# The last quad of w_out's sums on VectorE and its stores on ScalarE; the first weight split behind the third pair's even terms

## The chip, the cores and the metric

One core of a Trainium2 chip runs the whole kernel. The metric is the time of one execution on the device in microseconds. TensorE (PE) multiplies matrices; VectorE (DVE), ScalarE (ACT) and GpSimd (POOL) work on elements; SyncE (SP) and ScalarE issue most of the DMAs. Each engine takes its instructions in the order in which they were written; between engines there are semaphores.

## The reference

```python
B, H, S, D = 8, 8, 576, 64
scores = q @ k.T / sqrt(D)                 # per batch and head
ret = scores * Dmat[h]                     # Dmat = gamma[h] ** (i - j) for i >= j, else 0
x = (ret @ v).transpose(0, 2, 1, 3).reshape(4608, 512)
g, val = x @ w_gate, x @ w_val             # 512 -> 1536
out = (silu(g) * val) @ w_out              # 1536 -> 512, all float32
```

## The kernel before, in words

**Attention.** The 64 heads of all batches are worked in 32 pairs, each in chunks of 64 positions with a carried state. A `tick(t)` has TensorE's instructions for three pairs at once: `own_values(t-2)` (L481) needs the masked scores `ret` of pair t-2, `new_states(t-1)` is L490, `earlier_values(t-2)` (L500, L504) needs the carried states, and `scores(t-1)` (L511, L517) needs the transposed queries and keys, qT and kT. VectorE and ScalarE then do the element work of the tick, in this order: `even` (a copy, L528) and the scaling of keys (L459), the outputs of pair t-2 into x (`to_x`, L554 and L568), `ret` (L524), the last row of it (L532), the states (L534 to L539), qT and kT of pair t (L454). For the first four pairs (`hi == HP` in `tick`) the order is a little different: in a tick come scores and new states of pair t-1, then `masked(t-1)` with `even`, `ret` and states, then the values and outputs of pair t-2, then the transposes of pair t by TensorE (L440).

**Feed-forward network.** Tokens come in a first tile of 512 (`up0`, L650, and `down0`, L662) and four tiles of 1024. The tiles of 1024 use a fast scheme for products of 4 x 4 blocks with 26 multiplications and prepared sums: `up_step` (L870) runs 26 steps for each of three quads of the hidden dimension, `down_step` (L909) 26 steps. The sums of blocks of x are made by VectorE (`x_sums`), those of the up weights by GpSimd in the second tile (`w_sums` and `first_sums`), and each of these is then stored to DRAM from ScalarE's queue (L873), so that later tiles read it back. The operands of `down_step` are sums of blocks of w_out: `out_sums(qd)` makes them for quad `qd`, 24 sums of 128x256 by the table `OUT_SUMS`, and stores 26 blocks to the DRAM tensors `dn0` to `dn25` (L728). A sum is written to one of `sum_places` and its place comes free when its last use, often the store, is over. The places of quad 2 of w_out and some of `sum_places` are later used for the sums of x.

**Weights.** Weights are loaded as they are, 64-bit float numbers, into three raw buffers; `split` (ScalarE, L378 and L379) and `rounding` (VectorE, L391 and L392) turn a half of each into float32. `rounding(j)` calls `split(j + 1)`, and `split` issues the load of a further weight.

**Order around the change.** First come ticks 0 to 5 with the first `split` and `rounding`. Then a list `plan` merges `up0`, ticks 4 to 9, weight loads and the first groups of `out_sums` (a group is the sums for three stores). Then twelve `down0`, with tick 10 after the second, 11 after the fourth, 12 after the seventh and 13 after the ninth, and the remaining groups of `out_sums`: one after each of the first three `down0`, two after each later one. After the ninth, `first_sums(0, 0, 4)` makes the first sums of the up weights. Then `out0` copies the first tile's output and stores it from ScalarE's queue (L670), and the `up_step`s of the second tile begin. Before the change all sums of w_out are GpSimd's and all their stores are SyncE's.

A DMA increments one of eight completion semaphores. They are taken in turn by the DMAs of both queues, and a DMA is issued only when the one before it on its semaphore has landed.

Of the kernel before, what the change touches and what calls it, by code (L numbers as in the profile page):

```python
# [154 lines left out]
def kernel(  # L155
# [32 lines left out]
    nc = tc.nc  # L188
# [13 lines left out]
    TB = TW // 4  # L202
    NF = DF // P
    NQ = NF // 4
# [37 lines left out]
    rest = const.tile([P, 17920], F32, name="rest")  # L242
    raw_at, part_at, x0_at, dn_at, sum_at = 0, 6144, 8192, 10240, 16384
# [125 lines left out]
    def split(j):  # L369

        i, f = halves[j]
        bits = bits_of(i, f)
        top, ulp = [rest[:, part_at + 512 * (2 * n + j % 2) : part_at + 512 * (2 * n + j % 2 + 1)] for n in range(2)]
        blocks = lambda a: a.rearrange("p (c m) -> p c m", m=P)
        nc.scalar.activation(out=blocks(top), in_=bits[:, :, :, 1].bitcast(F32), func=AF.Prelu, scale=2.0 ** -112, alpha=2.0 ** 32)  # L378
        nc.scalar.activation(out=blocks(ulp.bitcast(I32)), in_=bits[:, :, :, 0].bitcast(U32), func=AF.Copy, scale=2.0 ** -29)  # L379
        parts[j] = top.bitcast(I32), ulp.bitcast(I32)  # L380
        if f and j // 2 + RAWS < len(order):
            load_w(j // 2 + RAWS)

    def rounding(j):

        i, f = halves[j]
        dst = weights[i][1][f].bitcast(I32)
        top, ulp = parts.pop(j)  # L390
        nc.vector.tensor_scalar(out=dst, in0=top, scalar1=3, scalar2=None, op0=ALU.logical_shift_left)  # L391
        nc.vector.tensor_tensor(out=dst, in0=dst, in1=ulp, op=ALU.add)  # L392
        if j + 1 < len(halves):
            split(j + 1)
# [200 lines left out]
    def tick(t, lo=HP, hi=NP, spread=False, then=None):  # L595
        go_on(len(pieces))
        if hi == HP:

            if lo <= t - 1 < hi:
                scores(t - 1, True)  # L600
                new_states(t - 1)
                for f in masked(t - 1):
                    f()
            if lo <= t - 2 < hi:
                own_values(t - 2)
                earlier_values(t - 2)
                to_x(t - 2)[0]()
            for f in transposes(t) if lo <= t < hi else ():
                f()
            return  # L610
        if lo <= t - 2 < hi:
            own_values(t - 2)
        if lo <= t - 1 < hi:
            new_states(t - 1)
        if lo <= t - 2 < hi:
            earlier_values(t - 2)
        if lo <= t - 1 < hi:
            scores(t - 1, t - 2 < lo)
        copies, *masks = masked(t - 1) if lo <= t - 1 < hi else (lambda: None,)
        keys, *new = transposes(t) if lo <= t < hi else (lambda: None,)  # L620
        outputs = to_x(t - 2)[0] if lo <= t - 2 < hi else lambda: None
        if t - 2 >= 0 and light(t - 2):
            pieces.append(lambda: (copies(), keys(), outputs()))
        else:
            pieces.extend([lambda: (copies(), keys()), outputs])
        pieces.extend(masks)
        pieces.extend(new)
        if then:
            pieces.append(then)
        if not spread:  # L630
            go_on(len(pieces))
# [33 lines left out]
    def out0():  # L665
        for i, bank in enumerate(banks):
            o = rest[:, part_at + 512 * i : part_at + 512 * (i + 1)]
            (nc.vector.tensor_copy if i > 1 else nc.scalar.copy)(out=o, in_=bank)
        for i in range(4):
            nc.scalar.dma_start(out=out[i * P : (i + 1) * P, :], in_=rest[:, part_at + 512 * i : part_at + 512 * (i + 1)])  # L670
# [5 lines left out]
    def add(eng, op, view, to=None):  # L676
        dst, srcs = view(int(op[1])) if to is None else to, [view(int(a)) for a in op[2:]]
        if op[0] == "neg":
            eng.tensor_scalar(out=dst, in0=srcs[0], scalar1=-1.0, scalar2=None, op0=ALU.mult)
        elif op[0] == "nad" and eng is nc.vector:  # L680
            eng.scalar_tensor_tensor(out=dst, in0=srcs[0], scalar=-1.0, in1=srcs[1], op0=ALU.mult, op1=ALU.subtract)
        elif op[0] == "nad":
            eng.tensor_tensor(out=dst, in0=srcs[0], in1=srcs[1], op=ALU.add)
            eng.tensor_scalar(out=dst, in0=dst, scalar1=-1.0, scalar2=None, op0=ALU.mult)
        else:
            eng.tensor_tensor(out=dst, in0=srcs[0], in1=srcs[1], op=ALU.add if op[0] == "add" else ALU.subtract)  # L686

    up_ops = [[dr.tile([P, 512], F32, name=f"up{qd}_{i}") for i in range(N)] for qd in range(NQ)]
    dn_ops = [dr.tile([P, 768], F32, name=f"dn{i}") for i in range(N)]

    sum_places = [rest[:, sum_at + TB * i : sum_at + TB * (i + 1)] for i in range(6)]
    more_places = [rest[:, raw_at + TB * i : raw_at + TB * (i + 1)] for i in range(16) if i % 4]

    events = []
    for line in OUT_SUMS:
        i, s = line.split("|")
# [2 lines left out]

    def out_sums(qd):

        place = {}

        def view(s):
            return w_dn[:, qd, s // 2, s % 2] if s < 8 else place[s]

        def used(e):
            return [e[1]] if e[0] is None else [int(a) for a in e[1][2:]]  # L710

        def release(k):

            for s in list(place):
                for e in events[k + 1 :]:
                    if s in used(e):
                        break
                    if s == e[0]:
                        sum_places.append(place.pop(s))
                        break  # L720
                else:
                    sum_places.append(place.pop(s))

        def do(k):
            e = events[k]
            if e[0] is None:
                _, slot, i = e
                nc.sync.dma_start(out=dn_ops[i][:, qd * TB : (qd + 1) * TB], in_=view(slot))  # L728
            else:
                new = sum_places.pop(0)  # L730
                add(nc.gpsimd, e[1], view, new)
                if e[0] in place:
                    sum_places.append(place[e[0]])
                place[e[0]] = new
            release(k)

        r, ends = [], [k for k, e in enumerate(events) if e[0] is None]
        for g in range(0, N, 3):
            lo, hi = ends[g - 1] + 1 if g else 0, ends[min(g + 2, N - 1)] + 1

            def group(lo=lo, hi=hi):
                for k in range(lo, hi):
                    do(k)

            r.append(group)
        return r
# [188 lines left out]

    for t in range(HP + 2):
        tick(t, 0, HP)
        if t == 2:
            split(0)

        for j in {2: (0,), 3: (1, 2), 4: (3, 4, 5)}.get(t, ()):
            rounding(j)
        if t == 3:
            load(HP)
        if t > 3:
            for f in range(2):
                up0(f, range(2) if t == 4 else range(2, HP))
# [6 lines left out]
        if t + AHEAD < NP:  # L954
            load(t + AHEAD)

    groups = [(qd, group) for qd in range(NQ) for group in out_sums(qd)]
    todo = [m for m in range(3, len(order))]
    plan = []

# [7 lines left out]
    for f in range(2, NF):  # L968
        round_until({4: 12, 6: 13, 8: 14, 9: 15, 10: 16, 11: 17}.get(f, f + 2))
        plan.append(lambda f=f: up0(f, range(HP)))  # L970
        if f - 1 in tick_at and f < NF - 1:
            plan.append(lambda t=tick_at[f - 1]: next_load(t))
        if f in tick_at:
            plan.append(lambda t=tick_at[f]: tick(t, HP, FIRST))
        if f >= NF - 2:

            plan.append(lambda t=tick_at[f]: next_load(t))
        for _ in range(0 if f == 9 else 3):
            if f >= (7, 10, NF)[groups[0][0]]:
                if f + 1 == NF and more_places:  # L980
                    plan.append(lambda places=more_places[:]: sum_places.extend(places))
                    more_places.clear()
                plan.append(lambda group=groups.pop(0)[1]: group())
    assert not todo
# [3 lines left out]
    for m, f in enumerate(down_order):  # L988
        down0(f)
        go_on(4)  # L990
        if m in tick_at:
            tick(tick_at[m], HP, FIRST, tick_at[m] + 1 < needed(1))
            go_on(1)
        if m == 8:
            first_sums(0, 0, 4)
        if m > 8:
            x_sums(1, 3 * (m - 9), min(3 * (m - 8), X_FIRST), True)
        for _ in range(min(1 if m < 3 else 2, len(groups))):
            groups.pop(0)[1]()
    out0()  # L1000
    x_sums(1, X_FIRST, X_FIRST_OF_ALL, True)
    done = FIRST
# [55 lines left out]
```

## Time and profile before

| | |
|---|---|
| median of 8 runs | 1079.23 us (1076.23 to 1083.83) |
| the profiled execution | 1083.83 us, of which the profile spans 1082.1 |
| TensorE busy | 1043.3 us (96%) |
| VectorE, ScalarE, GpSimd busy | 652.6, 271.5, 415.3 us |
| granted TensorE clock | 0.99 in the mean |
| DMA | 198.58 MB, 184 GB/s in the mean |

A row of the profile names the line, the engine, the operation, what is written and read, the number of instructions, then times. "SPq" and "ACTq" are DMA issues of SyncE and ScalarE. In a timeline the two numbers at the start are the start and the duration in microseconds from the start of the span, and the bracket at the end is the idle time before and what ended it. A row of several instructions has the start of the first.

### The profile page before, as it was taken

Reading aid. Unit: us, or ns where it says so; the run is one execution under the profiler, and the core shown is the slowest. Engines: PE = TensorE matmul, PEld = TensorE weight load, DVE = VectorE, ACT = ScalarE, POOL = GpSimd, SP = SyncE. Lnnn points to the kernel's source line nnn. Section 1 sums busy time; section 2 is a strip of 40 time slices with the busy share of each in tenths; the row PEclk is TensorE's granted clock in tenths of the full one; section 3 lists DMA queues with packets and bytes.
Section 4 is the critical chain, followed back from the end, with each engine's and each line's share of the span. In section 5 each row is a group of like instructions: output and inputs, shape, how many; then the busy total and the mean of one; then the engine's idle time right before and its main releaser. Section 6 shows DMA issues by size and latency. Waiting matters only on the chain.

```text
span 1082.1 us, 21481 instructions
## 1 busy us (share of the span) xinstructions
PE 1043.3 (96%) x8420; PEld 854.5 (79%) x8420; DVE 652.6 (60%) x1069; ACT 271.5 (25%) x578; POOL 415.3 (38%) x372
## 2 busy tenths in 40 slices
PE   6899999699999999999999999999999999999998
PEld 5445555488788788888888888888888888888887
DVE  4468755567879766754646869535267465244644
ACT  3355400124333211223232111122221012231110
POOL 5002359676464402741315025622151375122505
PEclk9999999799999999999999999999999999999999
DMA  9699774766576868767657778554564555555653
GB/s 260 179 279 240 211 189 143 216 190 187 158 209 184 251 143 247 213 180 196 154 165 214 180 204 231 155 152 135 153 177 150 161 177 154 154 149 159 184 162 98
DMA packets 300700, 198.58 MB, mean 184 GB/s; under 512 B 215352, under 2 KB 244056, under 8 KB 300600
## 3 DMA queue, kind: packets, MB, share of 16 engines
q1 hardware_dynamic: 268230, 159.16, 54.2%
q10 hardware_dynamic: 31954, 37.17, 10.4%
q8 instruction: 67, 1.10, 0.4%
q0 software_dynamic: 416, 0.89, 0.3%
q14 instruction: 33, 0.27, 0.1%
HBM read 157.04 MB, written 40.11 MB: 182 GB/s over the span
## 4 chain that ended last, share of the span: by engine, by line
PE 79%; POOL 6%; DMA 5%; DVE 5%; issue 2%; SPq 2%; ACT 1%; ACTq 0%; DVEq 0%; POOLq 0%
PE bankC L870 11%; PE bankB L870 11%; PE bankE L870 10%; PE bankA L870 10%; PE bankA L909 6%; PE bankE L909 6%; PE bankB L909 6%; PE bankC L909 6%; POOL rest L686 3%; DVE rest L810 2%; PE bankA L650 2%; PE bankC L650 2%; PE bankE L650 2%; PE bankB L650 2%; PE outer L504 1%
## 5 line engine op out<-in xcount | busy, mean ns | idle before, releaser
L810 POOL TENSOR_TENSOR rest<-rest 128x512 f32<-128x512 f32 x56 | 79.2, 1420 | 300.9 <-DVE rest L810 282.8
L885 ACT ACTIVATE io<-rest 128x256 f32<-128x256 f32 x180 | 75.0, 416 | 341.1 <-DVE rest L810 291.6
L870 PE MATMUL bankA<-rest,arena 128*128 128x256 f32 x544 | 130.6, 383 | 4.4 <-ACT rest L807 3.3
L870 PE MATMUL bankC<-rest,arena 128*128 128x256 f32 x544 | 129.2, 380 | 1.1 <-POOL arena L839 0.6
L686 POOL TENSOR_TENSOR arena<-arena 128x512 f32<-128x512 f32 (+1 forms) x72 | 115.2, 1612 | 28.2 <-DMA up<-arena 20.4
L870 PE MATMUL bankE<-rest,arena 128*128 128x256 f32 x512 | 122.6, 383 | 0.8 <-DVE rest L810 0.8
L686 POOL TENSOR_TENSOR rest<-rest 128x256 f32<-128x256 f32 (+1 forms) x86 | 81.4, 969 | 105.9 <-issue 64.8
L870 PE MATMUL bankB<-rest,arena 128*128 128x256 f32 x512 | 121.4, 380 | 0.4 <-DVE rest L810 0.4
L870 PEld LDWEIGHTS bankA<-rest,arena 128*128 128x128 f32 x544 | 103.8, 192 | 20.9 <-issue 5.5
L892 POOL TENSOR_TENSOR arena<-rest,io 128x256 f32<-128x256 f32 x72 | 52.0, 729 | 166.9 <-ACT io L885 166.9
L870 PEld LDWEIGHTS bankC<-rest,arena 128*128 128x128 f32 x544 | 102.8, 190 | 16.2 <-issue 1.2
L870 PEld LDWEIGHTS bankE<-rest,arena 128*128 128x128 f32 x512 | 98.0, 192 | 14.9 <-issue 1.1
L870 PEld LDWEIGHTS bankB<-rest,arena 128*128 128x128 f32 x512 | 96.9, 190 | 14.3 <-DVE rest L810 0.8
L810 DVE TENSOR_TENSOR rest<-bankB,rest 128x512 f32<-128x512 f32 x72 | 48.9, 687 | 66.2 <-PE bankB L870 48.2
L810 DVE TENSOR_TENSOR rest<-bankE,rest 128x512 f32<-128x512 f32 x72 | 48.8, 686 | 64.7 <-PE bankE L870 46.1
L810 DVE TENSOR_TENSOR rest<-bankC,rest 128x512 f32<-128x512 f32 x72 | 48.9, 687 | 63.4 <-PE bankC L870 43.5
L810 DVE TENSOR_TENSOR rest<-bankA,rest 128x512 f32<-128x512 f32 x72 | 48.8, 686 | 61.1 <-PE bankA L870 43.8
L888 DVE SCALAR_TENSOR_TENSOR arena<-rest,io 128x256 f32<-128x256 f32 x84 | 58.6, 702 | 11.7 <-ACT io L885 11.7
L909 PE MATMUL bankA<-arena 128*128 128x256 f32 x252 | 58.0, 380 | 1.3 <-DVE arena L686 1.3
L909 PE MATMUL bankB<-arena 128*128 128x256 f32 x252 | 58.3, 381 | 0.0
L909 PE MATMUL bankC<-arena 128*128 128x256 f32 x252 | 58.1, 380 | 0.0
L909 PE MATMUL bankE<-arena 128*128 128x256 f32 x252 | 57.9, 379 | 0.0
(179 smaller groups left out, 1630.1 us busy)
## 6 DMA issues: line engine op xcount, KB each, us to landing
arena<-up SPq DMA_DIRECT2D x234, 256.0 KB
arena<-dn SPq DMA_DIRECT2D x104, 384.0 KB
up<-arena ACTq DMA_DIRECT2D x78, 256.0 KB
dn<-rest SPq DMA_DIRECT2D x78, 128.0 KB
out_dram<-rest SPq DMA_DIRECT2D x32, 256.0 KB
qk<-in_q_dram SPq DMA_DIRECT2D x108, 72.0 KB
qk<-in_k_dram SPq DMA_DIRECT2D x108, 72.0 KB
v<-in_v_dram SPq DMA_DIRECT2D x58, 128.0 KB
```

The costliest lines, as they stand in the source:

```text
L504: nc.tensor.matmul(xr[half[hl]] if c + 1 == NC else xo[half[hl ^ c % 2 * exchange(i)], c // 2, c % 2], state[half[hl], c, :], s["qT"][half ...
L650: nc.tensor.matmul(bank, w_up[:, f // 4, gv, f % 4, c // 2, (c % 2) * P : (c % 2 + 1) * P], xs[0][:, c, :], start=(c == 0), stop=(c == HP ...
L686: eng.tensor_tensor(out=dst, in0=srcs[0], in1=srcs[1], op=ALU.add if op[0] == "add" else ALU.subtract)
L810: eng.tensor_tensor(out=at(op[1]), in0=at(op[2]), in1=at(op[3]), op=ALU.add if op[0] == "add" else ALU.subtract)
L870: nc.tensor.matmul(b[:, gv * TB : (gv + 1) * TB], w[:, gv, ts(c, P)], rhs[:, c, :], start=(opens and gv == 0 and c == 0), stop=(c == 1), s ...
L885: nc.scalar.activation(out=s, in_=src[:, 0:TB], func=AF.Silu, scale=-1.0 if negative else 1.0)
L888: return lambda: nc.vector.scalar_tensor_tensor(out=dst, in0=src[:, TB : 2 * TB], scalar=-1.0, in1=s, op0=ALU.mult, op1=ALU.mult)
L892: nc.gpsimd.tensor_tensor(out=dst, in0=src[:, TB : 2 * TB], in1=s, op=ALU.mult)
L909: nc.tensor.matmul(b[:, m * TB : (m + 1) * TB], lhs[:, qd, ts(m, P)], w[:, qd], start=(opens and qd == 0 and m == 0), stop=(qd == NQ - 1), ...
```

## The change

Two things are changed. First, `out_sums` of the last quad (`NQ - 1`) makes its sums on VectorE, into six places of its own, and stores them from ScalarE's queue; a group of it is placed after each of the first nine `down0`, and one group of the other quads after each `down0` while there are any. GpSimd gets six further places at the end of the plan, where it got twelve. Second, `split(0)` and `rounding(0)` stand in tick 3, behind `masked(2)`, and no longer at the end of tick 2. VectorE has three instructions fewer for a quad than GpSimd: a negated sum is one instruction there and two on GpSimd. The numbers of lines behind L603 grow by 3 to 7.

```diff
@@ tick, first four pairs
                 new_states(t - 1)
                 for f in masked(t - 1):
                     f()
+            if t == 3:
+                split(0)
+                rounding(0)
             if lo <= t - 2 < hi:
                 own_values(t - 2)
@@
-    sum_places = [rest[:, sum_at + TB * i : sum_at + TB * (i + 1)] for i in range(6)]
+    pool_places = [rest[:, sum_at + TB * i : sum_at + TB * (i + 1)] for i in range(6)]
     more_places = [rest[:, raw_at + TB * i : raw_at + TB * (i + 1)] for i in range(16) if i % 4]
+    vector_places = more_places[6:]
@@ out_sums
         place = {}
+        eng, queue, sum_places = ((nc.vector, nc.scalar, vector_places) if qd + 1 == NQ else (nc.gpsimd, nc.sync, pool_places))
@@ do
-                nc.sync.dma_start(out=dn_ops[i][:, qd * TB : (qd + 1) * TB], in_=view(slot))
+                queue.dma_start(out=dn_ops[i][:, qd * TB : (qd + 1) * TB], in_=view(slot))
             else:
                 new = sum_places.pop(0)
-                add(nc.gpsimd, e[1], view, new)
+                add(eng, e[1], view, new)
@@ first ticks
         tick(t, 0, HP)
-        if t == 2:
-            split(0)
-
-        for j in {2: (0,), 3: (1, 2), 4: (3, 4, 5)}.get(t, ()):
+
+        for j in {3: (1, 2), 4: (3, 4, 5)}.get(t, ()):
             rounding(j)
@@ plan
-    groups = [(qd, group) for qd in range(NQ) for group in out_sums(qd)]
+    groups = [(qd, group) for qd in range(NQ - 1) for group in out_sums(qd)]
+    last_groups = out_sums(NQ - 1)
@@
-                    plan.append(lambda places=more_places[:]: sum_places.extend(places))
+                    plan.append(lambda places=more_places[:6]: pool_places.extend(places))
@@ after each down0
-        for _ in range(min(1 if m < 3 else 2, len(groups))):
+        if groups:
             groups.pop(0)[1]()
+        if last_groups:
+            last_groups.pop(0)()
```

## The prediction

> **What bounds the kernel now.** I read the busy rows first (TensorE 96% of the span), then TensorE's own waits, since only its idle time can be won, then the stages, then each engine's timeline around the widest gap. TensorE's waits from 140 to 230 us:
>
> ```profile
> PE bankC L870 <- POOL arena L686: 7.0, 1, 7.0
> PE bankA L870 <- ACT rest L807: 3.3, 1, 3.3
> PE bankC L870 <- POOL arena L839: 0.6, 1, 0.6
> PE outer L511 <- DVE kT L454: 0.2, 1, 0.2
> ```
>
> Three gaps, 10.9 us, all at L870: the first ten steps of `up_step` for the second x tile. The table of stages shows what they cost (busy us and count of PE, PEld, DVE, ACT, POOL, then the granted clock, DMA share and GB/s):
>
> ```profile
> 138.00:150.00 12.00, 12.00 (x162) 6.35 (x160) 3.25 (x12) 1.15 (x2) 2.75 (x4) 1.00 1.15 227
> 150.00:176.00 26.00, 25.57 (x382) 14.86 (x382) 14.52 (x38) 0.00 (x0) 23.17 (x32) 1.00 0.50 164
> 176.00:187.00 11.00, 11.00 (x29) 5.16 (x28) 10.86 (x15) 1.17 (x2) 10.92 (x11) 1.00 0.37 124
> 187.00:220.00 33.00, 22.09 (x78) 17.50 (x77) 18.43 (x25) 6.01 (x13) 22.08 (x23) 0.79 0.72 211
> ```
>
> TensorE idles 10.91 us from 187 to 220 at a clock of 0.79, while from 150 to 176 it is full, GpSimd too (23.17 of 26), VectorE half empty and ScalarE empty. TensorE's timeline gives the loss:
>
> ```profile
> 187.86 1.89 PE L870 MATMUL bankB<-rest,arena 128*128 128x256 f32 x8
> 196.76 3.78 PE L870 MATMUL bankC<-x_odd,arena 128*128 128x256 f32 x8 [7.01 <-POOL arena L686]
> 206.86 3.41 PE L870 MATMUL bankA<-rest,arena 128*128 128x256 f32 x8 [3.33 <-ACT rest L807]
> 219.72 1.99 PE L870 MATMUL bankC<-rest,arena 128*128 128x256 f32 x8 [0.57 <-POOL arena L839]
> ```
>
> Step 0 starts at 186.14 and step 10 at 219.72: 33.6 us for ten steps, which follow each other every 1.73 us where nothing waits (17.3). So **16.3 us** are lost, 10.9 of waits and the rest in groups of eight that take 3.4 to 3.8 us after them. Why GpSimd is late:
>
> ```profile
> 177.12 8.85 POOL L686 TENSOR_TENSOR rest<-rest 128x256 f32<-128x256 f32 x8
> 195.45 2.93 POOL L686 TENSOR_TENSOR arena<-arena 128x512 f32<-128x512 f32 x2
> ```
>
> It is at the w_out sums until 195.45, and only then makes the weight sum that step 2 needs. The sums of quad 2 begin after quad 1's last, at about 172.4. The 3.3 us gap is ScalarE: its stores of the first output wait until 197.29 for a completion semaphore that SyncE's queue of w_out stores holds (data ready at 184.4), and step 0's bank is copied behind them.
>
> [...] eight GpSimd sums take 5.83 us at 156.6 and 8.85 at 177.1, where VectorE adds in SBUF without pause, and VectorE's 128x512 adds then take 1.2 us against 0.68 alone.[...] Here a w_out store lands in 1.9 us (issued 201.16, releases VectorE at 203.08) to 3.6 us (issued 148.33, releases GpSimd at 152.01, where the DMA share is over 1).[...]
>
> **The change by parts.** (1) Off GpSimd: quad 2's 24 sums, 27 instructions there, 172.4 to 196, 23.8 us. Off SyncE: 26 of the 60 stores that fill its queue from 147.53 to 202.58, so its next loads (202.68) start some 20 us earlier, beside TensorE's full stage and not in the up-steps. The weight sum of step 2 then follows quad 1 (about 173 to 178), long before 190; the stores of the first output no longer wait. What is late next is the chain store of step 0's weight, its landing, then six GpSimd sums to step 10. That store can be issued some 2.1 us after step 0 starts; the 3.1 us landing of 205.22, 5.5 of 206.57 and sums of 1.45 put step 10 at 17.5 us after step 0 against 17.3. **Gain 16.1 us.**
>
> (2) On VectorE: 24 instructions. An add of 128x256 there takes 0.41 us (L891), 0.9 where GpSimd competes; I take 0.77, half of a GpSimd sum of 0.72 longer. In sum 10 to 18 us, against VectorE's waits between 137.9 and 176 of 5.1, 3.1, 0.6, 0.9, 5.7 and 4.6 us (20.0). As work alone it fits. But VectorE runs in order, and the change puts *waits* ahead of pair work. Six places serve 24 sums, so the seventh waits for the first store to land, and it stands before `to_x(8)`, `ret` and states of pair 9, kT of pair 10:
>
> ```profile
> 147.10 1.12 ACTq L301 DMA_DIRECT2D vl<-in_v_dram  x1
> 149.28 0.22 DVE L532 TENSOR_TENSOR ret_last<-outer,last_near 128x64 f32<-128x64 f32 x1
> 151.86 0.73 DVE L454 STREAM_TRANSPOSE kT<-qk 128x576 f32<-128x576 f32 x1
> 152.65 0.27 PE L511 MATMUL outer<-qT,kT 64*64 64x64 f32 x2 [0.20 <-DVE kT L454]
> ```
>
> TensorE waits for kT already here, by 0.2 us: no slack. ScalarE is at pair loads until 148.22, so the first store lands at 148.3 + 3.6 = 151.9. Then: sum 0.4, outputs 0.9, `ret` and its last row 0.75 (153.95, against 149.4), states 2.8 (between 1.9 with GpSimd idle and 3.1 beside it), qT 0.7, four more sums that stand between qT and kT 3.1, kT 0.7: 161.2. TensorE starts the scores at 161.2 and not 152.65: **loss 8.5 us**. Ends: landing 1.9 and sums of 0.41 give 157.1, loss 4.5; landing 4.6 (seven stores in flight together) and sums of 0.9 give 10.5.
>
> Tick 12 is covered: TensorE reaches it at 163.87 + 8.5 = 172.4, and its pair work, five sums later, is done by about 172. Tick 13 is not. Before its `ret(11)` stand four sums; one waits for a ScalarE store whose completion semaphore was last used by one of SyncE's stores at the end of quad 1. Quad 1 ends at 172.4 now; 13 VectorE sums meet it, at (8.85 - 5.83)/8 = 0.38 each, so 177; SyncE's store 1.9 and ScalarE's 0.45 + 1.9 give 181.3, the sum 0.4, outputs and `ret` 1.7: 183.4. TensorE arrives at 173.66 + 8.5 = 182.2: 1.2 us, and 1.3 more for the states. **Loss 2.5 us**, ends 0 and 6. The clock:[...] I take nothing; upper end 3.4.
>
> (3) ScalarE's 26 stores at 0.45 us are 12 us in a queue that has no work from 149.4 to 183.76; behind them are a weight negation and the copies of the first output, needed at 194 then. Nothing, unless the last stores slip beyond 194; the end would be 3 us. GpSimd keeps 12 of its 18 places for two thirds of its sums, which costs nothing as long as the 1.9 us landings hold.
>
> (4) `split(0)` and `rounding(0)` move from tick 2 to tick 3 behind `masked(2)`. ScalarE copies `even` at 21 and not 24.63, since no weight is awaited before it; VectorE's pair terms come some 3 us earlier, its first rounding some 3 us later (21.3 to 24), the next two about 2 earlier, still before L650 needs them at 34.65. SyncE's weight load (30.23) and pair loads behind it go out up to 1.7 us earlier. TensorE:
>
> ```profile
> 28.43 0.57 PE L481 MATMUL outer<-ret,v 64*64 64x64 f32 x23 [0.95 <-DVE rest L568]
> 32.01 0.35 PE L481 MATMUL outer<-ret,v 64*64 64x64 f32 x9 [3.01 <-issue]
> ```
>
> The 0.95 us goes, but the next gap stands within 32 equal matmuls and waits for no data: "issue". I hold that it ends at the same time, so 0; ends 1.5 gained if it moves along, 1 lost if the earlier loads delay it.
>
> **Sum:** -16.1 + 8.5 + 2.5 + 0 = -5.1 us. The profiled execution took 1083.83 (span 1082.1, 1.7 around it), so 1078.7; it was the slowest of eight, and the median 1079.23 becomes **1074.1**.
>
> **Rivals.** *A, full cover:* the stores land fast, VectorE's gaps take all: 1079.2 - 15.7 = 1063.5. For it, 20 us of gaps; against it, the order: the waits stand ahead of kT. *B, slower:* VectorE held by stores. With 3.6 us for every landing the second stall is about 7 us, the first 9.5, and two half-clock windows bring 3.4: 19.9 against 16.1, 1083.0. It decides from the point where stalls in ticks 11 to 13 exceed 16.1 us. Against it, the 1.9 us landings once the loads are over. *C, equal:* stalls of 13 to 19 us return what is won, 1079.
>
> **Numbers.** A measurement of this kernel can tell about 0.3% (3.2 us) from no change. Forecast 0.56 (1070 to 1078, a sixth of it within 0.3%), A 0.16, B 0.14, C 0.14. Faster 0.47 + 0.16 = 0.63, same 0.09 + 0.14 = 0.23, slower 0.14. The range leaves out the best half of A and the worst of B: 1065 to 1082.
>
> **What would show it.** Right: TensorE has no gap at the first L870 groups, all at 1.9 us; a gap of 4.5 to 10.5 us at L481, L504 and L511 near 150 to 161, released by VectorE, a smaller one near 182; VectorE waits for DMA stores; step 0 at about 197. Wrong: no gap near 150 (A), one over 6 us near 182 or a clock under 1 from 150 to 185 (B), a new wait for GpSimd or ScalarE after step 0, or a start that moves TensorE's first L650 from 34.65 by over 1 us.

## The result, and the profile after

The changed kernel takes **1073.49 us** in the median of 21 runs (1070.52 to 1078.34), the kernel before beside it 1079.41 in 58: ratio **0.9947, interval 0.9935 to 0.9958**, 5.7 us less (7.0 to 4.5). The forecast was 1074.1. The profiled execution took 1070.52 us, its span is 1068.8. It is the fastest of its runs as the profile of before is one of the slowest, so the two spans differ by 13.3 us where the medians differ by 5.9: of the two traces only stretches are compared below, not spans.

TensorE's waits from 140 to 230 us in the profile after (total, times, longest):

```profile
PE outer L481 <- DVE ret_last L532: 5.0, 1, 5.0
PE outer L511 <- DVE kT L454: 2.3, 1, 2.3
PE outer L500 <- PE outer L481: 0.2, 1, 0.2
```

The three gaps at the up-steps (L870, now L876) are gone, and two others have come, both in tick 11 and both ended by VectorE. The stages, in the same columns as those of before:

```profile
138.00:150.00 12.00, 6.98 (x24) 2.87 (x26) 4.15 (x14) 0.00 (x0) 2.76 (x4) 0.91 1.01 264
150.00:176.00 26.00, 23.69 (x304) 14.25 (x301) 21.07 (x43) 0.00 (x0) 19.88 (x25) 0.78 0.64 203
176.00:187.00 11.00, 10.82 (x90) 5.47 (x89) 8.36 (x21) 1.15 (x2) 3.26 (x2) 1.00 0.96 217
187.00:220.00 33.00, 33.00 (x140) 26.23 (x139) 26.41 (x36) 9.93 (x20) 16.64 (x12) 1.00 0.53 174
```

The idle time and the low clock have moved from the last row (before: 22.09 busy, clock 0.79) to the first two. The up-steps are full at clock 1.00. TensorE's timeline, with steps 0, 2 and 10:

```profile
192.27 1.89 PE L876 MATMUL bankA<-rest,arena 128*128 128x256 f32 x8
...
195.73 1.89 PE L876 MATMUL bankC<-x_odd,arena 128*128 128x256 f32 x8
...
209.79 1.99 PE L876 MATMUL bankC<-rest,arena 128*128 128x256 f32 x8
```

Ten steps take 209.79 - 192.27 = 17.5 us. GpSimd's timeline shows why:

```profile
168.93 1.45 POOL L689 TENSOR_TENSOR arena<-arena 128x512 f32<-128x512 f32 x1
183.74 1.58 POOL L689 TENSOR_TENSOR arena<-arena 128x512 f32<-128x512 f32 x1 [13.37 <-DVE arena L689]
```

It is through with quad 1 at 168.93 and makes a weight sum then (before: 195.45, step 2 waiting for it), and the gap behind it is a wait for VectorE. What VectorE does with the work, in its timeline:

```profile
147.29 0.79 DVE L689 TENSOR_TENSOR rest<-rest 128x256 f32<-128x256 f32 x1 [3.71 <-DMA dn<-rest]
...
148.93 0.68 DVE L524 TENSOR_TENSOR ret<-inner,near 128x512 f32<-128x512 f32 x1
...
152.55 2.97 DVE L689 TENSOR_TENSOR rest<-rest 128x256 f32<-128x256 f32 x4
155.45 0.77 DVE L454 STREAM_TRANSPOSE kT<-qk 128x576 f32<-128x576 f32 x1
```

A sum waits 3.71 us for a store to land and holds `ret` behind it, and four sums of 0.74 us stand between qT and kT. And TensorE's timeline where it waits, with the first groups behind it:

```profile
149.79 1.14 PE L481 MATMUL outer<-ret,v 64*64 64x64 f32 x32 [5.02 <-DVE ret_last L532]
...
156.26 0.37 PE L511 MATMUL outer<-qT,kT 64*64 64x64 f32 x2 [2.31 <-DVE kT L454]
...
157.53 2.07 PE L665 MATMUL bankA<-rest,arena 128*128 128x512 f32 x2
...
162.19 1.02 PE L665 MATMUL bankE<-rest,arena 128*128 128x512 f32 x2
```

The group of L665 at 157.53 takes 2.07 us where the one at 162.19 takes 1.02: the two waits are paid a second time in half-clocked work. The granted clock is 0.50 from 147.91 to 161.56, for 13.65 us. In quarters of that length, with one ahead and one behind and the columns of the stages:

```profile
144.50:147.91 3.41, 0.27 (x1) 0.00 (x0) 0.62 (x1) 0.00 (x0) 0.83 (x2) 1.00 0.97 324
147.91:151.33 3.42, 1.54 (x56) 1.54 (x60) 3.31 (x12) 0.00 (x0) 3.25 (x5) 0.50 0.61 203
151.33:154.74 3.41, 2.63 (x56) 2.26 (x48) 3.38 (x7) 0.00 (x0) 3.41 (x5) 0.50 0.68 225
154.74:158.15 3.41, 1.89 (x37) 1.64 (x38) 1.94 (x4) 0.00 (x0) 3.33 (x5) 0.50 0.71 235
158.15:161.56 3.41, 3.41 (x5) 1.35 (x4) 3.41 (x11) 0.00 (x0) 3.32 (x5) 0.50 0.47 158
161.56:164.98 3.42, 3.42 (x9) 1.52 (x8) 3.31 (x8) 0.00 (x0) 3.25 (x6) 1.00 0.71 234
```

It falls after a stretch in which TensorE is busy for 0.27 us, within the first wait, and comes back after one in which it is busy for all 3.41 us.

### The profile page after: what moved, and what is told of

It reads as the page before. It is cut to its first block, busy times and chain, and to the rows that moved or that the text cites. A ratio compares the mean times of both kernels' runs of the same rounds, so it can differ in the third digit from the quotient of the medians.

```text
span 1068.8 us, 21457 instructions
## 1 busy us (share of the span) xinstructions
PE 1038.6 (97%) x8420; PEld 851.2 (80%) x8420; DVE 663.5 (62%) x1093; ACT 272.0 (25%) x578; POOL 395.7 (37%) x345
## 3 DMA queue, kind: packets, MB, share of 16 engines
q10 hardware_dynamic: 35698, 40.58, 11.4%
## 4 chain that ended last, share of the span: by engine, by line
PE 87%; DVE 5%; DMA 4%; issue 1%; POOL 1%; ACT 1%; SPq 0%; ACTq 0%; DVEq 0%; POOLq 0%
PE bankC L876 11%; PE bankE L876 11%; PE bankB L876 11%; PE bankA L876 11%; PE bankA L915 6%; PE bankB L915 6%; PE bankC L915 6%; PE bankE L915 6%; DVE rest L816 2%; PE bankA L653 2%; PE bankC L653 2%; PE bankE L653 2%; PE bankB L653 2%; PE outer L504 2%; PE outer L481 2%
## 5 line engine op out<-in xcount | busy, mean ns | idle before, releaser
L876 PE MATMUL bankC<-rest,arena 128*128 128x256 f32 x544 | 129.2, 380 | 0.5 <-DVE rest L816 0.5
L876 PE MATMUL bankA<-rest,arena 128*128 128x256 f32 x544 | 129.0, 380 | 0.5 <-DVE rest L816 0.4
L876 PE MATMUL bankE<-rest,arena 128*128 128x256 f32 x512 | 121.5, 380 | 0.8 <-DVE rest L816 0.8
L876 PE MATMUL bankB<-rest,arena 128*128 128x256 f32 x512 | 121.4, 380 | 0.4 <-DVE rest L816 0.4
L876 PEld LDWEIGHTS bankA<-rest,arena 128*128 128x128 f32 x544 | 102.9, 190 | 16.0 <-issue 1.3
L876 PEld LDWEIGHTS bankC<-rest,arena 128*128 128x128 f32 x544 | 102.8, 190 | 15.6 <-issue 1.2
L876 PEld LDWEIGHTS bankE<-rest,arena 128*128 128x128 f32 x512 | 96.8, 190 | 14.7 <-issue 1.2
L876 PEld LDWEIGHTS bankB<-rest,arena 128*128 128x128 f32 x512 | 97.0, 190 | 14.3 <-DVE rest L816 0.8
L689 POOL TENSOR_TENSOR rest<-rest 128x256 f32<-128x256 f32 (+1 forms) x66 | 65.8, 1018 | 100.7 <-issue 60.1
L894 DVE SCALAR_TENSOR_TENSOR arena<-rest,io 128x256 f32<-128x256 f32 x84 | 58.2, 698 | 11.7 <-ACT io L891 11.7
```

Of the source, the lines that this page charges most:

```text
L876: nc.tensor.matmul(b[:, gv * TB : (gv + 1) * TB], w[:, gv, ts(c, P)], rhs[:, c, :], start=(opens and gv == 0 and c == 0), stop=(c == 1), s ...
L894: return lambda: nc.vector.scalar_tensor_tensor(out=dst, in0=src[:, TB : 2 * TB], scalar=-1.0, in1=s, op0=ALU.mult, op1=ALU.mult)
```

## The experiments

The theory: the up-steps win 16 us because GpSimd is free, and tick 11 loses 11 of it because VectorE's sums, waiting for a place and standing ahead of kT, come before TensorE's operands. The first rival: most of the 5.7 us is the other edit, the later split. To compare runs I take two stretches from TensorE's timeline, which begin over 100 us behind the start: **A** from the start of the last `down0` group (bankE) ahead of tick 11 to the start of up-step 0, and **B** from step 0 to step 10.

| kernel | A, us | B, us | A + B less before's | measured by ratio, us |
|---|---|---|---|---|
| before (mean of 4 traces) | 37.1 | 33.5 | 0 | 0 |
| the change | 48.5 | 17.5 | -4.6 | -5.7 (-7.0 to -4.5) |
| e1 sums and stores only | 49.2 | 17.5 | -3.9 | -2.8 (-4.6 to -1.0) |
| e2 split only | 36.5 | 34.6 | +0.5 | -0.9 (-2.8 to +1.1) |
| e3 twelve places | 43.0 | 18.0 | -9.6 | -11.2 (-14.0 to -8.3) |
| e4 no stores | 45.0 | 17.5 | -8.1 | -12.4 (-15.3 to -9.6) |
| e5 twelve places, kT first | 40.5 | 18.2 | -11.9 | -13.9 (-16.4 to -11.4) |
| e6 six places, kT first | 49.7 | 18.2 | -2.7 | -5.0 (-6.4 to -3.7) |
| e7 stores on SyncE | 63.4 | 17.5 | +10.3 | +7.8 (+5.5 to +9.9) |
| e9 as e5, sums two groups later | 41.2 | 17.7 | -11.7 | -13.2 (-16.6 to -9.7) |

The last column is the ratio less one, times 1079.5 us; the other columns come from one trace each. The traces of before have 37.1 and 33.6, 36.4 and 34.1, 37.6 and 33.0, 37.2 and 33.5.

**e1, one half of the change.** All of the sums, places and stores; the split stays in tick 2.

```diff
-            if t == 3:
-                split(0)
-                rounding(0)
...
+        if t == 2:
+            split(0)
-        for j in {3: (1, 2), 4: (3, 4, 5)}.get(t, ()):
+        for j in {2: (0,), 3: (1, 2), 4: (3, 4, 5)}.get(t, ()):
```

(against the changed kernel)

> Only the sums and stores of the last quad are moved; the first split stays in tick 2. Theory of the prediction (all of the change's effect lies between tick 11 and up-step 10, the start is worth nothing): ratio to before 0.995, as for the whole change; first L650 group at 34.6 us as before, gap of some 5 us at L481 after tick 10 and 2 us at L511, no gap at the first up-steps. Rival (the 4.8 us by which the changed kernel's profile is ahead at its first L653 come from the split's place): this part alone gives what is left, 0.998 to 1.000.

Measured: 1077.3 us, ratio 0.9974 (0.9957 to 0.9991). B is 17.5 us as with the whole change, and tick 11 has gaps of the same kind (4.9, 0.7 and 2.9 us). So the gain at the up-steps and the loss at tick 11 belong to this half. The ratio lies nearer the rival's 0.998 than the theory's 0.995, which its interval leaves out: the whole change gains 2.9 us more than this half, though the intervals reach 1.8 and 1.2 us to either side.

**e2, the other half**, against the kernel before.

```diff
+            if t == 3:
+                split(0)
+                rounding(0)
...
-        if t == 2:
-            split(0)
-        for j in {2: (0,), 3: (1, 2), 4: (3, 4, 5)}.get(t, ()):
+        for j in {3: (1, 2), 4: (3, 4, 5)}.get(t, ()):
```

> Only the first split and rounding are moved to tick 3; the sums are all GpSimd's as before. Theory of the prediction: 1.000, within 1.5 us, the gap of 3 us that is put down to issue within L481 still there near 32 us. Rival (the split's place gives the 4.8 us at the start): 0.995 to 0.997, first L650 group near 30 us and no gap within L481.

Measured: 1077.99 us, ratio 0.9992 (0.9974 to 1.0010): alone it can't be told from nothing. The up-steps keep their gaps (8.1 and 5.0 us). e1 and e2 together say only that the later split is worth between 0 and about 3 us; e8, e10 and e11 go on with that.

**e3, twelve places for VectorE**, none of them handed to GpSimd. No store has to land before the thirteenth sum.

```diff
-    vector_places = more_places[6:]
+    vector_places = more_places[:]
...
-                if f + 1 == NF and more_places:
-                    plan.append(lambda places=more_places[:6]: pool_places.extend(places))
-                    more_places.clear()
```

> The changed kernel, but VectorE's sums have twelve places and GpSimd keeps its first six (they took six and twelve), so VectorE's first twelve sums wait for no store. Theory (the loss at tick 11 is the wait for the first store, with what is queued behind it): gap at L481 gone, at L511 at most 2.5 us, no half clock after it; 7 us less than the changed kernel, ratio to before 0.988. Rival (the loss is the work of the sums on VectorE itself): as the changed kernel, 0.995. Rival 2 (GpSimd with six places falls behind and is late at the up-steps again): a gap at L876 for GpSimd, 0.995 or more.

Measured: 1068.35 us, ratio 0.9896 (0.9870 to 0.9923). TensorE's waits in the same window:

```profile
PE outer L511 <- DVE kT L454: 2.9, 1, 2.9
PE outer L481 <- DVE ret_last L532: 1.0, 1, 1.0
```

The 5.0 us have become 1.0, and A is 5.5 us shorter. **The wait for the store to land was about half of the loss** (5.5 of 11.4 us), and GpSimd does with six places: B stays at 18.0. The gain is less than the 7 us expected, and the expectation "no half clock" failed:

```profile
150.45:153.86 3.41, 1.14 (x37) 0.96 (x38) 2.44 (x5) 0.00 (x0) 3.32 (x5) 1.00 0.66 221
153.86:157.28 3.42, 3.42 (x5) 1.35 (x4) 3.42 (x6) 0.00 (x0) 3.34 (x5) 0.50 0.95 310
```

TensorE is busy for 1.14 of 3.41 us, a third, and the clock of the next 3.42 us is 0.50.

**e4, no stores of the last quad.** Its sums are made, but never reach DRAM; SyncE's stores of quad 1 write their block twice, so that as many bytes go out.

```diff
-                queue.dma_start(out=dn_ops[i][:, qd * TB : (qd + 1) * TB], in_=view(slot))
+                if qd == 1:
+                    queue.dma_start(out=dn_ops[i][:, TB:].rearrange("p (c x) -> p c x", c=2),
+                                    in_=view(slot).unsqueeze(1).to_broadcast([P, 2, TB]))
+                elif qd == 0:
+                    queue.dma_start(out=dn_ops[i][:, 0:TB], in_=view(slot))
```

> The changed kernel without the 26 stores from ScalarE: quad 1's stores from SyncE write their block into quad 2's columns too, so as many bytes go to DRAM but VectorE's sums wait for no landing (the sums of quad 2 are made and thrown away). Theory (waits for stores make the loss): no gap at L481 near 150, at L511 at most 2.5 us, tick 13 without a gap; ratio 0.987 to 0.989. Rival (the sums' own time on VectorE): 0.995. Rival of full cover: 0.985.

Measured: 1067.66 us, ratio 0.9885 (0.9858 to 0.9911). Waits of 2.6 us at L481 and 1.4 at L511 stay although no sum waits for a place: in this trace the keys of pair 10 landed at 145.4 and not 142.7, and the sums stand between them and `ret`. Its time agrees with e3's within the intervals. It gains 4.3 us more than its two stretches show; where these lie stays open.

**e5, kT before the four sums.** On top of e3, one more piece of pair work is done behind each `down0`.

```diff
         down0(f)
-        go_on(4)
+        go_on(5)
```

> The change with twelve places for VectorE, and one more piece of pair work behind each down0, so that kT comes before the four sums that stood between qT and kT. With twelve places alone TensorE waited 1.0 us for ret_last, 0.5 for a state and 2.9 for kT, and 1.4 us went at half clock, 5.8 in all. If the order of the sums and kT makes the 2.9 us, that gap falls under 0.5, and with it most of the half-clocked groups: 3 to 4 us off the 1068.4 of twelve places, 1064.5 to 1065.5, ratio 0.9865. Rival: kT waits for the DMA of the queries and keys or for VectorE's earlier work anyway, then the gap stays above 2 us and the ratio is that of twelve places alone, 0.9896.

Measured: **1065.78 us**, ratio 0.9871 (0.9848 to 0.9894), and TensorE's waits from 138 to 230:

```profile
PE outer L481 <- DVE ret_last L532: 1.8, 1, 1.8
PE bankC L876 <- POOL arena L845: 0.7, 1, 0.7
PE bankC L876 <- DVE rest L816: 0.5, 1, 0.5
PE outer L504 <- DVE state L539: 0.5, 1, 0.5
```

The wait for kT is gone, so its cause was the order. Some half clock stays: from 150 to 176 us the mean clock is 0.95, and the 32 matmuls of L504 at 149.54 take 1.97 us where those at 164.10 take 1.11. A falls by 2.5 us; the two intervals of e3 and e5 overlap, so for the time itself this step isn't proved. The version beats the kernel before by 13.9 us, and its interval lies wholly below that of the change.

**e6, the same reorder with six places**: `go_on(5)` in the change itself.

> The change itself, six places, with kT before the four sums and nothing else. If the two stalls are independent, the 5.0 us wait for ret_last stays, the 2.3 us wait for kT goes, and some of the 4.0 us of half clock with it: 2.3 to 4 us off 1073.5, so 1069.5 to 1071, ratio 0.991 to 0.9925. Rival: the wait for the store's place alone makes both, kT then waits as long as before: ratio 0.9947.

Measured: 1074.51 us, ratio 0.9954 (0.9941 to 0.9966): nothing gained. The trace shows neither expectation but a third thing:

```profile
PE outer L481 <- DVE ret_last L532: 9.6, 2, 5.0
```

The 2.3 us at kT are gone as forecast, and the first L665 groups behind it take 1.12 and 1.02 us (the change: 2.07 and 1.91), but L481 now waits *twice*. VectorE's timeline ahead of the second:

```profile
173.06 0.88 DVE L689 TENSOR_TENSOR rest<-rest 128x256 f32<-128x256 f32 x2 [3.40 <-DMA dn<-rest]
174.74 0.42 DVE L689 TENSOR_TENSOR rest<-rest 128x256 f32<-128x256 f32 x1 [0.80 <-DMA dn<-rest]
177.13 0.42 DVE L689 TENSOR_TENSOR rest<-rest 128x256 f32<-128x256 f32 x1 [1.96 <-DMA dn<-rest]
```

Six us of waits for stores, ahead of `ret` for tick 13; TensorE waits 4.57 us there. This is the second stall of the prediction. With the change itself TensorE comes to tick 13 at 179.8, 2.4 us after `ret_last` is done (177.4); with e6 it comes at 174.7. **The first stall hid the second**, and what is won at the first is given back. The last of the three stores also lands 1.8 us later than in the change (177.13 against 175.35): ScalarE's queue issues one store between 165.4 and 172.9, and goes on when SyncE's last w_out store is issued (172.4), as the prediction had it. More places take both stalls away (e5 has no wait for a store on VectorE).

**e7, SyncE stores the last quad.**

```diff
-        eng, queue, sum_places = ((nc.vector, nc.scalar, vector_places) if ...
+        eng, queue, sum_places = ((nc.vector, nc.sync, vector_places) if ...
```

> The change with one part undone: VectorE makes the sums of the last quad, but SyncE stores them. SyncE's queue then holds quad 1's stores, which wait for GpSimd, and quad 2's in turn, so a place of VectorE's comes free only when GpSimd's earlier sums are done: the wait for the first store grows, TensorE's gap at L481 from 5.0 to some 8 to 12 us, with more gaps at later ticks, and the next loads go out near 190 again and not 171. 1077 to 1082, ratio 0.998 to 1.003. Rival: SyncE's queue keeps up, because there is one store of each quad in turn and GpSimd is no slower; then ScalarE's part was of no use and the ratio is 0.9947.

Measured: **1087.29 us**, ratio 1.0072 (1.0051 to 1.0092), slower than both. SyncE's queue, then TensorE:

```profile
144.18 52.44 SPq L734 DMA_DIRECT2D dn<-rest  x60
```

```profile
164.85 1.14 PE L481 MATMUL outer<-ret,v 64*64 64x64 f32 x32 [19.28 <-DVE ret_last L532]
```

VectorE's first place comes free only behind GpSimd's stores in the same queue: 17.3 us of waiting, 19.3 for TensorE, where 8 to 12 were expected. So ScalarE's queue carries the change. B is 17.5 us here too, but SyncE's 60 stores end at 196.6, 11 us before step 0 (207.96), so this run does not tell GpSimd's free time from a free SyncE queue. In the profile of before, SyncE's stores waited 27.7 us for GpSimd's sums between 140 and 215 us, so the late queue goes back in part to the same work.

**e8, e10 and e11: the kernel before, unedited, for its start.**

> The kernel before once more, for a second look at its start. In the profile of before TensorE's first L650 group starts at 34.65 us, with a gap of 3.0 us within the equal matmuls of L481 that no data ends; with the sums alone moved it started at 31.36 and with the split alone at 31.25. If that gap is chance and not the place of the split, this look gives something between 30 and 35 us with nothing changed, most likely near 31.3; if it belongs to the early split, 34 to 35 again. The ten up-steps take 33 to 35 us either way.

> The kernel before, another look at the start. Seven traces with the late split have TensorE's first L653 group at 29.9 to 31.25 us (mean 30.7), three without it at 31.36, 31.99 and 34.65. If the late split is worth about 1 us, this one starts L650 above 31.3; if the start is chance alone, anywhere from 29.9 to 32.

> As the look before it: above 31.3 us if the late split is worth about 1 us at the start, from 29.9 if it is chance.

TensorE's first L650 starts at 31.99 (e8), 34.55 (e10) and 35.38 us (e11). With 34.65 (before) and 31.36 (e1), the early split has 31.4 to 35.4, mean 33.6, in five traces; the eight with the late split have 29.9 to 31.3, mean 30.7. They don't overlap, if only by 0.1 us. The clock parts them better: over the first 40 us its mean is 0.96 in before, e1 and e8, and 1.00 in the change, e3, e6 and e7 (0.96 in e5). Of the others, e10 and e11 have the 32 matmuls of L504 ahead of L650 in 1.95 us, e2, e4 and e9 in 1.13, and 30 of L517 before them in 0.67 (28 in 1.02 in e1). So it is hardly chance alone. TensorE's timeline of e10:

```profile
31.76 0.49 PE L481 MATMUL outer<-ret,v 64*64 64x64 f32 x9 [3.00 <-issue]
```

This gap, within 32 equal matmuls and ended by no data, is 2.7 to 3.0 us in three of the five and absent in two; with the late split it is 0.8 to 1.5 us where it is there at all. What makes it isn't settled. Nor do 2.9 us at L650 reach the end whole: e2 has only 0.9. The four traces of before are of executions of 1080.6 to 1083.8 us, all above the median of 1079.4, so they may show more loss at the start than most executions have.

**e9, the sums two groups later.** On top of e5:

```diff
-        if last_groups:
+        if last_groups and m > 1:
```

> Twelve places, kT before the sums, and the groups of the last quad after the third to the eleventh down0 instead of the first to the ninth, so that no sum of it stands ahead of ret(9). In the trace of twelve places with kT first TensorE still waits 1.8 us for ret_last and 0.5 for a state; three sums of 1.1 us stand ahead of them. If they are the cause, TensorE waits under 1 us there and the stretch from tick 11 to step 0 shrinks from 40.5 us to 38 to 39.5: 1064 to 1065.5, ratio 0.985 to 0.987. Rival: the sums that are pushed back stand before the sums of x and the copies of the first output, or their stores stand ahead of ScalarE's copies at step 0, and what is won is lost at the up-steps: 1066 to 1069, ratio 0.988 to 0.990.

Measured: 1064.97 us, ratio 0.9878 (0.9846 to 0.9910), not to be told from e5. The wait for `ret_last` is gone, but at tick 13 a state is 1.4 us late and step 0 waits 0.4 us for ScalarE's copy of the first output: A is 41.2 us, not shorter. The time fits the theory's range, A does not; the rival is right that what is won is lost later, but most of it is lost at tick 13 and not at the up-steps. Ahead of the late state VectorE works without a pause from 148.3, so a sum moved from one tick is late in another.

## Why the prediction was right, and where its terms were off

- **The gain at the up-steps, 16.1 us: right.** B went from 33.5 us to 17.5, 16.0. Cause as given for the 7.0 us gap: GpSimd's weight sum no longer follows quad 2 (168.93 against 195.45). It is not that TensorE now comes to step 0 later: with e9 A is only 4.1 us longer, and B is 17.7. The 3.3 us gap of ScalarE's late stores is gone as forecast: before, each of the four stores of the first output waited at a semaphore, the first until 197.2, and their issues took 7.19 us from 197.29; now they take 2.65 us from 190.89. (In the trace of before the w_out stores land on eight semaphores in turn.) No run takes SyncE's part in it from GpSimd's.
- **The first stall, 8.5 us: right, by its own measure.** The scores of tick 11 start 12.5 us after the last `down0` group and not 3.6 as before: 8.9 us later. Of these 7.3 are gaps (5.0 + 2.3) and some 1.6 half-clocked work between them. The first ScalarE store was forecast to land after 3.6 us; it was issued at 143.72 and VectorE went on at 147.29, 3.6. Beside the pair loads (DMA share 1.01) the 3.6 us measured in before were the number to take. qT, sums and kT took 0.7, 2.97 and 0.77 against 0.7, 3.1 and 0.7. e3 takes away the first gap by its cause, e5 the second.
- **The clock, 0 (upper end 3.4): wrong.** A grew by 11.4 us, of which 7.3 are gaps; some 4.1 us are work at half clock, 2.5 of them behind the scores. The upper end is two stretches of 3.4 us at half clock; in the trace of before the clock is 0.50 for 3.41 us from 32.31 and from 206.39 and for 10.24 us from 192.73. To take nothing for the first stall was the author's estimate, and two measurements speak against it. First, by the prediction's own times TensorE would stand still at L481 from 149.97 to 153.95, 4.0 us; it stood for 5.0, up to 149.79, and the clock fell within them, at 147.91. Second, it fell behind shorter waits too: in e3, where the longest is 2.9 us, it was 0.50 after 3.41 us with 1.14 us (33%) of work. A clock under 1 before 185 was also the prediction's sign of B, and it came without B.
- **The second stall, 2.5 us (0 to 6): 0 in the change**, since gaps and half clock brought TensorE to tick 13 late enough. e6 shows that the mechanism is there: 4.57 us.
- **The start, 0 (-1.5 to +1): too small.** The whole change gains 2.9 us more than e1, e2 alone 0.9, and the kernels with the late split but e4 lie 1.1 to 2.5 us below their stretches. The step that failed is "I hold that it ends at the same time": where the "issue" gap is there, it ends at 31.8 to 32.6 us with the early split and at 28.5 to 29.5 with the late one; why stays open. L650 moved by more than 1 us, which the prediction named as a sign against it.
- **The sum.** Stalls and clock: 11.4 us against 11.0. Up-steps 16.0 against 16.1. That leaves -4.6. The other -1.1 I put down to the start, but it is a remainder that no run isolates, and the interval of the ratio (-7.0 to -4.5) just holds -4.6. The errors cancelled by luck (clock +4.1, second stall -2.5, gaps 7.3 for 8.5): the total was hit closer than its parts.
- **Rivals.** A, full cover (1063.5; its sum takes off 15.7, the gain of 16.1 gives 1063.1), fell; it is what e5 and e9 nearly reach, after the places and the order are mended. B, slower, fell for the change, and its turning point held: with e7 the stalls pass 16.1 us (A is 26.3 longer) and the kernel is slower.

## What to carry to other kernels

Work given to an engine with idle time is free only if it can also *wait* there for free (the wait for the first store made 5.5 of the 11.4 us in e3): count the buffers between the engine and its stores before counting its busy share, and look at what stands behind the waiting instruction. When a stall is taken away, look one tick on: a second, hidden by the first, may give all of it back, as e6 did (a wait of 4.6 us). And a producer's stores belong in a queue that holds no slower producer's stores ahead of them (e7: 17 us).

## What was not expected of the hardware

The clock was 0.50 for 3.41 and 10.24 us at a time in before and for 13.65 us in the change. In e9 slow groups followed a wait of 1.4 us: behind the one that ends at 172.10 the first L665 groups take 2.07 and 1.36 us and the next 1.02. TensorE was busy for 0.27 us (the change) and 1.14 us (e3) of the 3.41 us ahead of such a stretch. In before it was busy for 1.73 of the 3.42 us from 25.48, and the next 3.41 us still had a clock of 1.00. These are single traces with modelled busy times, too few for a rule. Within 32 equal matmuls that wait for no data a gap of up to 3.0 us came and went between executions of one kernel (0 in e8, 3.0 in e10).
